# A third split product in two feature blocks of eight, kept high parts made at the ends of cycles, and four early transforms one product later

## Chip, cores, metric

One core of one Trainium2 chip runs the whole program. The metric is the device time of the program in microseconds; the smaller the better. Three runs of the kernel before gave 1777.51, 1778.03 and 1778.36 us, with a median of 1778.03 us.

## What is computed

The reference takes the real part of a two-dimensional Fourier transform of each of 8 sequences and runs every row of the result through a two-layer network with a hard swish between the layers:

```python
X = np.fft.fft(x, axis=1)          # x: 8 x 3008 x 256, fp32
X = np.fft.fft(X, axis=2)
x = X.real.astype(np.float32).reshape(8 * 3008, 256)
h = x @ w_in                       # 256 x 2048
g = h * np.clip(h + 3.0, 0.0, 6.0) / 6.0
out = g @ w_out                    # 2048 x 256
```

## The kernel before

**Tiling.** The 8 sequences are taken as 4 pairs (`NP`). The tokens of a pair are cut into 12 chunks (`NCK`), so there are 48 chunks; they are numbered 0 to 47 here. A chunk has 256 columns, the last of each pair (11, 23, 35, 47) has 192. The 2048 hidden features are cut into 8 feature blocks (`NF`) of 256. A **step** is one chunk with one feature block: 384 steps.

**A step.** TensorE makes the hidden values (`passes`, L717: split fp32 data in the tiles `KQ` and `KW`, fp32r matmuls), ScalarE and VectorE make the gate from them (`relu` L791, `other_sign` L751, `gate` L794, into `A`), GpSimd sums quarters of it (`combine`, L809, into `c`), and TensorE makes the second layer (`mlp2`, L865, into the PSUM tiles `acc`). The second layer is a 2x2 block product in seven products (a Strassen-like scheme): products 0, 1 and 2 take the gate itself, 3 to 6 take the sums `c`. So there are seven products to a step.

**Plain and split products.** A product in fp32 is one call and stands as two matmuls with two weight loads in the trace. From chunk 8 on (`CHUNK2`), products 0 and 1 of each step are split instead: the moving side is cut into a high, a low and a remaining part, and so is the weight, and three fp32r matmuls add up to the product. `split_gates` (L882) makes the moving parts in the tile `J`: ScalarE writes the high part (L886) and copies it into a PSUM bank (L891), VectorE writes the other two (L892, L893). In feature block 4 (`THIRD`), product 2 is split as well, in every chunk from 8 to 47: `split_third` (L896) does the same on one product's 256 columns (L900, L903, L904, L905) into `J3`.

**The weights' parts.** The second layer's weights of products 0 and 1 (and 2 in block 4) lie in `GH[fc]`, the others in `G` and `G2`. `split_weights` (L910) writes the low and remaining parts into `GK`. The high part takes the place of the fp32 weight in `GH`: `keep_high` (L921) copies `GH` into a PSUM bank (L924) and multiplies it back (L926), both on ScalarE. That can be done for a block when chunk 7 has used its fp32 weight, and has to be done before chunk 8 uses it.

**The order of the work.** The order on every engine is written out by hand in the main loop at the end of the kernel function. One turn of that loop is a **cycle**; from chunk 8 on a cycle is one step long. A cycle starts with the odd half of the hidden values (`odd_half`), then the first product, then the even half of the next unit (`passes(nx, 0)`), the gates, and the rest of the products. `products(n)` emits the next n products; of the last ones, `behind_it` come after the transform that stands in some cycles (`stage1`, L327, and `stage1_quarters`, the Fourier transform along the sequence, 8 matmuls of K=47). A second transform (`stage2`, L563, 8 short matmuls) stands in other cycles. High parts are made after the first product of the cycle before (`flush(high_of)`, `third_high`), other parts at the end of it (`third_others`). `keep_high` is called in the middle of a cycle, at most once in one, not in cycles with a transform, and not together with `split_weights`.

**PSUM banks.** Eight banks: four for `acc`, two (`a0`, `a1`) for the hidden values `u`, and `y0` and `y1`. `y0` holds the second sign `v` of the gate, the copies of `split_third`, and one half of a transform; `y1` holds the copies of `split_gates`, the bank of `keep_high` and `split_weights`, and the other half of a transform (`bank`, `other_bank`). While `keep_high` holds `y1`, `split_gates` goes to `y0` (`lent`).

Of the kernel before, what the change touches and what calls it, by code (L numbers as in the profile page):

```python
# [60 lines left out]
def kernel(  # L61
# [10 lines left out]
    nc = tc.nc  # L72
# [56 lines left out]
    CHUNK2, NFR = 8, 2  # L129
    THIRD = (4,)  # L130
    SPLIT = CHUNK1 * NF - 2
# [5 lines left out]
    F1 = consts.tile([P, 5 * PB], F32, name="F1")  # L137
    FI = consts.tile([P, NIX + 1 + P], F32, name="FI")
    IX = FI[:, 0:NIX].bitcast(I32)
# [4 lines left out]
    G = consts.tile([P, 6 - NFR, NF, P], F32, name="G")  # L144

    def split_products(fc):
        return NFR + (fc in THIRD)

    GH = [consts.tile([P, split_products(fc), P], F32, tag=f"GH{fc}", name="GH") for fc in range(NF)]
    G2 = {fc: consts.tile([P, P], F32, tag=f"G2{fc}", name="G2") for fc in range(NF) if fc not in THIRD}  # L150

    def weight(i, fc):
        if i == NFR and fc in G2:
            return G2[fc][:]
        return GH[fc][:, i] if i <= NFR else G[:, i - NFR - 1, fc]
    half = consts.tile([P, 1], F32, name="half")
# [673 lines left out]
    def split_of(ch, fc):  # L830
        return ch.n_all >= CHUNK2

    def order_of(ch, fc):

        if not split_of(ch, fc):
            return [[(i, None)] for i in range(7)]
        high, others = ([(i, j) for i in range(NFR)] for j in (HIGH, OTHERS))
        rest = [[(i, ALL if i < split_products(fc) else None)] for i in range(NFR, 7)]
        if ch.final and fc >= NF - LAST:
            return [high, others] + [rest[i - NFR] for i in (3, 5, 6, 4, 2)]  # L840
# [7 lines left out]
    def mlp2(ch, fc, lo, hi):  # L848
# [8 lines left out]
        for i, parts in (x for part in order[lo:hi] for x in part):  # L857
# [3 lines left out]
            for j in parts or (None,):  # L861
                assert (j is None) != (weight(i, fc).dtype == F32R)
                w = weight(i, fc) if not j else GK[fc][:, j - 1, i]
                x = moving[i] if j is None else J3[:, j, 0:ch.n] if i == NFR else parts_tile(ch, fc)[:, j, i, 0:ch.n]
                nc.tensor.matmul(o, w, x,  # L865
                                 start=(fc == 0 and i % 2 == 0 and j in (None, 0)), stop=(fc == NF - 1),
                                 skip_group_check=True)
# [42 lines left out]
    def split_weights(fc):  # L910

        low, rest = (GK[fc][:, k] for k in range(2))
        ps = bank([P, split_products(fc), P], "high")
        nc.scalar.mul(low, GH[fc][:], HIGH_PART)
        nc.vector.tensor_scalar(ps[:], low.bitcast(F32), 1.0 / EPS, None, op0=AL.mult)
        nc.vector.scalar_tensor_tensor(low, GH[fc][:], (1.0 + EPS) / EPS, ps[:], op0=AL.mult, op1=AL.subtract)
        nc.vector.scalar_tensor_tensor(ps[:], ps[:], -EPS, low.bitcast(F32), op0=AL.mult, op1=AL.add)
        yield
        nc.vector.tensor_scalar(rest, ps[:], 1.0 / (1.0 + EPS), None, op0=AL.mult)

    def keep_high(fc):  # L921

        ps = bank([P, split_products(fc), P], "high")
        nc.scalar.copy(ps[:], GH[fc][:])  # L924
        GH[fc] = consts.tile([P, split_products(fc), P], F32R, tag=f"GH{fc}", name="GH")
        nc.scalar.mul(GH[fc][:], ps[:], HIGH_PART)  # L926
        yield

# [173 lines left out]
    def join(j):  # L1102
# [7 lines left out]

        outs = GH[2 * n + i][:, 0:NFR], G[:, B12 - NFR - 1:B22 - NFR:B22 - B12, 2 * n + i]
        for h, o in enumerate(outs):
# [3 lines left out]
    def mix_w_out(j):  # L1116

        g = {i: G[:, i - NFR - 1, 2 * j:2 * j + 2, :] for i in range(NFR + 1, 7)}
        tt = nc.gpsimd.tensor_tensor
# [4 lines left out]
        for k in range(2):  # L1124
            tt(weight(2, 2 * j + k), g[5][:, k], GH[2 * j + k][:, B21], op=AL.subtract)

# [30 lines left out]


    def load_table():
        nc.sync.dma_start(out=F1[:], in_=c_stage1[:, 8 * PB:13 * PB])  # L1160
# [14 lines left out]
    load_w(0, nc.sync)  # L1175
    nc.scalar.dma_start(out=F[:], in_=c_stage1[:, 0:8 * PB])
    nc.scalar.dma_start(out=FI[:], in_=c_stage1[:, 13 * PB:])
    zero = QN[PB:PX, 2]
# [125 lines left out]
    def beside():  # L1304
# [5 lines left out]
        for t, gr in ((2, 2), (10, 3)):  # L1310
            put(t, load_t, gr)
        put(2, spread_half, halves[0], 1)
        put(5, load_table)
        put(NF - 1, close_w)
# [40 lines left out]
    def open_slots():  # L1355
        nonlocal A, GK
# [3 lines left out]
        GK = [slots.tile([P, 2, split_products(fc), P], F32R, tag=f"GK{fc}", name="GK") for fc in range(NF)]  # L1360

# [4 lines left out]

    epool = jpool = KW = A = GK = J = J3 = None
    steps = [(p, ck, fc) for p in range(NP) for ck in range(NCK) for fc in range(NF)]
# [256 lines left out]
    seed(units[1])  # L1625
    weights_of, rested, kept = list(range(NF)), 0, 0

# [3 lines left out]

    thirds = [s for s in gates_of if steps[s][2] in THIRD]
    third = []

    def third_high():

        if thirds and not third and thirds[0] <= now[0] + 1:
            ch, fc = chunk(thirds.pop(0))
# [50 lines left out]
    while done < len(stream):  # L1689
# [18 lines left out]
        third_high()  # L1708
        if not un:
            third_others()  # L1710

# [56 lines left out]
        flush(high_of)  # L1768
        third_others()
        for gen in parts:  # L1770
            next(gen, None)
# [112 lines left out]
```

## Time and profile before

| what | value |
| --- | --- |
| median of three runs | 1778.03 us |
| the profiled execution, whole | 1779.34 us |
| its span in the trace | 1777.5 us |
| TensorE busy | 1764.3 us |
| VectorE busy | 1494.5 us |
| ScalarE busy | 1411.4 us |
| GpSimd busy | 1312.7 us |
| granted clock of TensorE | 0.999 |

The profiled execution took 1.8 us more than its span and 1.3 us more than the median of the runs. TensorE's matmuls overlap in the trace, and their ends are modelled, so its busy time is close to the whole span also where it runs below its best. What a step costs is read better from the distance between the starts of two cycles: the first matmul of the odd half (L717 with 127 rows) marks the start of each.

### The profile page before, as it was taken

The numbers are of one execution on the slowest core, as the hardware profiler recorded it, in microseconds if no ns is written. First come the engines' busy times: TensorE is split into PE (matmuls) and PEld (weight loads), VectorE is DVE, ScalarE is ACT, GpSimd is POOL, SyncE is SP. The second block draws the span as 40 slices with busy tenths as digits, with TensorE's granted clock in tenths as the row PEclk, the third lists the DMA queues.
The fourth block names the chain that finished last, engine by engine and source line by source line (L and its number), as shares of the span: only waits on it lengthen the run. The fifth ranks groups of instructions, "written<-read, shape, count | busy, mean of one in ns | idle before, by whom it ended". The sixth has DMA issues, their size and how long they took to land.

```text
span 1777.5 us, 30218 instructions
## 1 busy us (share of the span) xinstructions
PE 1764.3 (99%) x9632; PEld 1518.3 (85%) x9632; DVE 1494.5 (84%) x2868; ACT 1411.4 (79%) x2573; POOL 1312.7 (74%) x1474
## 2 busy tenths in 40 slices
PE   8999999999999999999999999999999999999998
PEld 6688888888988888888998888888899888888897
DVE  8988676668988888888898888888899888888887
ACT  6556666678888888888888888888888888888885
POOL 5687777776678787886768878887766766776675
PEclk9999999999999999999999999999999999999999
DMA  8433332312113222121112222321111111101101
GB/s 281 121 93 99 103 78 70 85 37 51 37 48 81 71 64 78 47 73 43 30 44 64 70 78 57 86 64 37 48 36 34 37 21 48 41 19 45 21 13 34
DMA packets 160811, 110.39 MB, mean 62 GB/s; under 512 B 122562, under 2 KB 141344, under 8 KB 160652
## 3 DMA queue, kind: packets, MB, share of 16 engines
q1 hardware_dynamic: 151900, 82.22, 18.5%
q0 software_dynamic: 7504, 25.65, 4.7%
q8 instruction: 76, 1.25, 0.3%
q14 instruction: 83, 0.68, 0.1%
q10 hardware_dynamic: 1248, 0.59, 0.1%
HBM read 71.93 MB, written 36.79 MB: 61 GB/s over the span
## 4 chain that ended last, share of the span: by engine, by line
PE 95%; DVE 2%; ACT 2%; issue 0%; DMA 0%; another core or an unknown queue 0%; DVEq 0%; ACTq 0%
PE acc L865 58%; PE u L717 27%; PE ps L563 2%; PE ps L327 2%; PE acc L819 1%; PE v L613 1%; PE u L613 1%; ACT t L791 1%; PE spare L1138 0%; DVE v L751 0%; PE ps L526 0%; PE ps L395 0%; PE awake L1165 0%; DVE J L892 0%; ACT PM L1069 0%
## 5 line engine op out<-in xcount | busy, mean ns | idle before, releaser
L865 PE MATMUL acc<-c,G 128*128 128x256 f32 (+1 forms) x3008 | 766.7, 376 | 0.0
L717 PE MATMUL u<-KQ,KW 128*128 128x512 f32 (+7 forms) x2376 | 743.8, 426 | 1.0 <-ACT s L741 0.6
L809 POOL TENSOR_TENSOR c<-A 128x512 f32<-128x512 f32 (+1 forms) x359 | 453.9, 1264 | 337.3 <-PE acc L865 328.5
L865 PEld LDWEIGHTS acc<-c,G 128*128 128x128 f32 x3008 | 533.1, 189 | 80.3 <-issue 12.8
L717 PEld LDWEIGHTS u<-KQ,KW 128*128 128x128 f32 (+1 forms) x2376 | 426.1, 189 | 67.0 <-ACT s L741 3.0
L791 ACT ACTIVATE t<-u,half 128x512 f32<-128x512 f32 (+1 forms) x384 | 261.9, 682 | 169.9 <-PE u L717 111.7
L791 ACT ACTIVATE t<-v,half 128x512 f32<-128x512 f32 (+1 forms) x384 | 262.3, 683 | 106.1 <-DVE v L751 104.5
L751 DVE SCALAR_TENSOR_TENSOR v<-s,u 128x512 f32<-128x512 f32 (+1 forms) x360 | 247.0, 686 | 117.5 <-ACT t L791 111.6
L809 POOL TENSOR_TENSOR c<-c,A 128x256 f32<-128x256 f32 (+1 forms) x359 | 260.4, 725 | 28.2
L809 POOL TENSOR_TENSOR c<-A,c 128x256 f32<-128x256 f32 (+1 forms) x359 | 260.2, 725 | 28.2
L794 DVE SCALAR_TENSOR_TENSOR A<-t,v 128x512 f32<-128x512 f32 (+3 forms) x481 | 250.2, 541 | 36.7 <-ACT t L791 34.1
L865 PE MATMUL acc<-J,GK 128*128 128x256 f32 (+1 forms) x1340 | 270.7, 322 | 1.4 <-DVE J L905 0.8
L892 DVE SCALAR_TENSOR_TENSOR J<-high,A 128x512 fp32r<-128x512 f32 (+1 forms) x315 | 211.2, 670 | 55.8 <-ACT high L891 45.4
L794 DVE SCALAR_TENSOR_TENSOR A<-t,u 128x512 f32<-128x512 f32 (+3 forms) x481 | 248.4, 537 | 0.0
L732 ACT ACTIVATE u<-QN,WN 128x512 f32<-128x512 f32 (+1 forms) x324 | 224.8, 694 | 0.0
L865 PEld LDWEIGHTS acc<-J,GK 128*128 128x128 f32 x1340 | 204.7, 189 | 17.5 <-DVE J L893 1.6
L893 DVE SCALAR_TENSOR_TENSOR J<-high,A 128x512 fp32r<-128x512 f32 (+1 forms) x315 | 210.5, 668 | 0.0
L886 ACT ACTIVATE J<-A 128x512 fp32r<-128x512 f32 (+1 forms) x315 | 193.4, 614 | 0.0
L891 ACT COPY high<-J 128x512 f32<-128x512 f32 (+1 forms) x315 | 185.2, 588 | 4.9 <-DVE KQ L893 2.4
L741 ACT COPY s<-u 128x512 f32<-128x512 f32 (+2 forms) x315 | 180.3, 572 | 9.5 <-PE u L717 8.3
L865 PE MATMUL acc<-A,G 128*128 128x256 f32 (+1 forms) x630 | 184.6, 375 | 0.0
L865 PEld LDWEIGHTS acc<-J,GH 128*128 128x128 f32 x670 | 125.8, 189 | 24.1
(184 smaller groups left out, 1808.5 us busy)
## 6 DMA issues: line engine op xcount, KB each, us to landing
out_dram<-o SPq DMA_DIRECT2D x744, 32.0 KB
T<-in_c_stage_dram SPq DMA_DIRECT2D x26, 512.0 KB
g<-zd SPq DMA_DIRECT2D x42, 256.0 KB
zd<-z SPq DMA_DIRECT2D x48, 192.0 KB
QN<-qd SPq DMA_DIRECT2D x43, 128.0 KB
xt<-in_x_dram SPq DMA_DIRECT2D x21, 256.0 KB
st<-in_moe_w_out_dram POOLq DMA_DIRECT2D x7, 512.0 KB
xt<-in_x_dram SPq DMA_DIRECT2D x17, 192.0 KB
```

Of the source, the lines that this page charges most:

```text
L717: nc.tensor.matmul(un.wide(un.u[:]) if un.joint else un.u[:, i, 0:un.nq], un.weights(j, blk, i, rows), un.moving(j, blk, rows), start=Fals ...
L732: nc.scalar.activation(un.wide(un.u[:]), un.wide(row), AF.Identity, scale=WN[:, f:f + 1])
L741: copy(un.wide(un.s[:]), un.wide(un.u[:]))
L751: nc.vector.scalar_tensor_tensor(v, s, -2.0, u, op0=AL.mult, op1=AL.add)
L791: nc.scalar.activation(t, h, AF.Relu, bias=half[:], scale=scale)
L794: nc.vector.scalar_tensor_tensor(dst, t, 1.0, h, op0=AL.min, op1=AL.mult)
L809: (eng or nc.gpsimd).tensor_tensor(out, in0, in1, op=AL.add)
L865: nc.tensor.matmul(o, w, x, start=(fc == 0 and i % 2 == 0 and j in (None, 0)), stop=(fc == NF - 1), skip_group_check=True)
L886: nc.scalar.mul(high, a, 1.0 - EPS / 2.0)
L891: nc.scalar.copy(ps, high.bitcast(F32))
L892: nc.vector.scalar_tensor_tensor(low, ps, -1.0, a, op0=AL.mult, op1=AL.add)
L893: nc.vector.scalar_tensor_tensor(rest, ps, 1.0 + EPS, a, op0=AL.mult, op1=AL.subtract)
```

## The change

The change has five parts.

1. `THIRD` goes from block 4 to blocks 3 and 5, and a chunk that is the last of its pair has no third split product (`third_of`). So the third split products are those of blocks 3 and 5 in the 36 chunks from 8 on that aren't last, 72 in all, in place of 40 (block 4 in all 40 chunks).
2. `GH` holds two products for every block, `G` holds the other five, and the third product's weight parts lie in `GK3`, made by `split_third_weights` after the other weights. `split_weights` and it share `split_parts`.
3. `keep_high` takes `y0` in place of `y1`, is called at the end of a cycle, up to twice, and may start when two products of chunk 7's step are done in place of all seven. `split_gates` isn't moved to `y0` for it any more.
4. Before step 62 a transform stands before the last product of its cycle, not before the last two (`behind_it`).
5. To make room in SBUF: the row that `split_q` sends out lies in `QN`, and the index and sign columns `FI` are loaded a second time into `signs` at step 2 (`load_index`, one DMA on SyncE's queue), since the first copy now lies in a pool that is closed early.

```diff
-    THIRD = (4,)
+    THIRD = (3,5)
...
+    def third_of(ch, fc):
+        return split_of(ch, fc) and fc in THIRD and not ch.last
...
-        if fc in THIRD:
-            rest = rest[1:3] + rest[0:1] + rest[3:]
+        rest = [[(i, None)] for i in range(NFR, 7)]
+        if third_of(ch, fc):
+            rest = rest[1:3] + [[(NFR, ALL)]] + rest[3:]
         order = [high] + rest[:2] + [others] + rest[2:]
...
+    def split_third_weights(fc):
+        yield from split_parts(weight(NFR, fc), bank([P, P], "high")[:], *(GK3[fc][:, j] for j in range(3)))
...
     def keep_high(fc):
 
-        ps = bank([P, split_products(fc), P], "high")
+        ps = ps_u.tile([P, NFR, P], F32, tag="y0", name="high")
         nc.scalar.copy(ps[:], GH[fc][:])
-        GH[fc] = consts.tile([P, split_products(fc), P], F32R, tag=f"GH{fc}", name="GH")
+        GH[fc] = consts.tile([P, NFR, P], F32R, tag=f"GH{fc}", name="GH")
         nc.scalar.mul(GH[fc][:], ps[:], HIGH_PART)
-        yield
...
-        ch.row = qpool.tile([P, TB], F32, tag="row", name="row")
+        ch.row = QN[:, ch.n_all % 4]
...
+    def load_index():
+        nonlocal FI, IX
+        FI, IX = signs, signs[:, 0:NIX].bitcast(I32)
+        nc.sync.dma_start(out=FI[:], in_=c_stage1[:, 13 * PB:13 * PB + NIX + 1])
...
     def third_others():
+        third_high()
         for gen in third:
             next(gen, None)
...
-        if kept < NF and not stages and not ends and done >= 7 * ((CHUNK2 - 1) * NF + kept - SPLIT) + 7:
-            splitting, kept = keep_high(kept), kept + 1
-            next(splitting)
-        elif weights_of and not stages and not ends and not closing and rested >= 3:
-            splitting, rested = split_weights(weights_of.pop(0)), 0
+        if weights_of and not stages and not ends and not closing and rested >= 3:
+            (f, fc), rested = weights_of.pop(0), 0
+            splitting = f(fc)
             next(splitting)
         lent[0] = splitting is not None
-        behind_it = 1 if any(s - 1 in middle_fns for s in begun) else 2
+        behind_it = 1 if any(s - 1 in middle_fns or s < CHUNK2 * NF - 2 for s in begun) else 2
...
         third_others()
+        for _ in range(2):
+            if kept < NF and not stages and not ends and done >= 7 * ((CHUNK2 - 1) * NF + kept - SPLIT) + NFR:
+                keep_high(kept)
+                kept += 1
```

Three places show how instructions move. The first is ScalarE around the start of chunk 8, before the change. `COPY high<-GH` and `ACTIVATE GH<-high` are one `keep_high`, `J<-A` and `high<-J` the split of the gates, `t` the two `relu`, `s` and `u` the hidden values of the next step.

```order
L741 COPY s<-u 128x512
L791 ACTIVATE t<-v,half 128x512
L924 COPY high<-GH 128x384
L926 ACTIVATE GH<-high 128x384
L891 COPY high<-J 128x512
L732 ACTIVATE u<-QN,WN 128x512
L791 ACTIVATE t<-u,half 128x512
L886 ACTIVATE J<-A 128x512
L791 ACTIVATE t<-v,half 128x512
L741 COPY s<-u 128x512
L924 COPY high<-GH 128x256
L926 ACTIVATE GH<-high 128x256
```

The same place on ScalarE after the change, from chunk 8's first step on:

```order
L733 COPY s<-u 128x512
L783 ACTIVATE t<-v,half 128x512
L889 COPY high<-J 128x512
L724 ACTIVATE u<-QN,WN 128x512
L927 COPY high<-GH 128x256
L929 ACTIVATE GH<-high 128x256
L927 COPY high<-GH 128x256
L929 ACTIVATE GH<-high 128x256
L783 ACTIVATE t<-u,half 128x512
L884 ACTIVATE J<-A 128x512
```

Before, the last four of the eight `keep_high` stand in the first four cycles of chunk 8, each ahead of `high<-J` and the next `u`; after, the last two stand behind `u` in the first of these cycles, the other six stand earlier, and the following cycles have none.

The second place is TensorE at the first transform after the hidden values are split, before (`ps` are the two banks of the transform, `y` its data):

```order
L865 MATMUL acc<-A,GH 128x256
L865 MATMUL acc<-A,G_112 128x256
L327 MATMUL ps_1871<-y,F_97 64x512
L327 MATMUL ps_1872<-y,F_97 64x512
L327 MATMUL ps_1871<-y,F_97 64x512
L327 MATMUL ps_1872<-y,F_97 64x512
L865 MATMUL acc<-c,G 128x256 x2
L717 MATMUL u<-KQ,KW 128x256 x6
```

The same place after:

```order
L863 MATMUL acc<-A,GH 128x256
L863 MATMUL acc<-A,G 128x256
L863 MATMUL acc<-c,G 128x256
L319 MATMUL ps_1860<-y,F_97 64x512
L319 MATMUL ps_1861<-y,F_97 64x512
L319 MATMUL ps_1860<-y,F_97 64x512
L319 MATMUL ps_1861<-y,F_97 64x512
L863 MATMUL acc<-c,G 128x256
```

One product `acc<-c,G` has moved from behind the transform to the front of it; the same happens at three more transforms and at no others.

The third place is ScalarE in a late chunk, before, around the third product of block 4 (`J<-A 128x256` and `high<-J 128x256`):

```order
L791 ACTIVATE t<-u,half 128x512
L886 ACTIVATE J<-A 128x512
L900 ACTIVATE J<-A 128x256
L791 ACTIVATE t<-v,half 128x512
L741 COPY s<-u 128x512
L891 COPY high<-J 128x512
L732 ACTIVATE u<-QN,WN 128x512
L903 COPY high<-J 128x256
```

After, from the second half of block 3's set to just ahead of block 5's:

```order
L783 ACTIVATE t<-v,half 128x512
L733 COPY s<-u 128x512
L889 COPY high<-J 128x512
L724 ACTIVATE u<-QN,WN 128x512
L901 COPY high<-J 128x256
L783 ACTIVATE t<-u,half 128x512
L884 ACTIVATE J<-A 128x512
L783 ACTIVATE t<-v,half 128x512
L733 COPY s<-u 128x512
L889 COPY high<-J 128x512
L724 ACTIVATE u<-QN,WN 128x512
L783 ACTIVATE t<-u,half 128x512
```

The set of two small operations stands once in a chunk before, in the cycle of block 3; after, it stands twice, in the cycles of blocks 2 and 4, and the cycle between (from the first `t<-u` of these rows to the last `u`) has none.

More of the change, by code (lines that the diff above doesn't have):

```diff
@@ L143 @@
     WN = consts.tile([P, NFC], F32, name="WN")
[L144 to L150, printed above, removed]
+    G = consts.tile([P, 7 - NFR, NF, P], F32, name="G")
+    GH = [consts.tile([P, NFR, P], F32, tag=f"GH{fc}", name="GH") for fc in range(NF)]
     def weight(i, fc):
-        if i == NFR and fc in G2:
-            return G2[fc][:]
-        return GH[fc][:, i] if i <= NFR else G[:, i - NFR - 1, fc]
+        return GH[fc][:, i] if i < NFR else G[:, i - NFR, fc]
     half = consts.tile([P, 1], F32, name="half")
@@ L837, in order_of @@
         high, others = ([(i, j) for i in range(NFR)] for j in (HIGH, OTHERS))
-        rest = [[(i, ALL if i < split_products(fc) else None)] for i in range(NFR, 7)]
         if ch.final and fc >= NF - LAST:
-            return [high, others] + [rest[i - NFR] for i in (3, 5, 6, 4, 2)]
-        if fc in THIRD:
-            rest = rest[1:3] + rest[0:1] + rest[3:]
+            return [high, others] + [[(i, None)] for i in (3, 5, 6, 4, 2)]
+        rest = [[(i, None)] for i in range(NFR, 7)]
+        if third_of(ch, fc):
+            rest = rest[1:3] + [[(NFR, ALL)]] + rest[3:]
         order = [high] + rest[:2] + [others] + rest[2:]
@@ L861, in mlp2 @@
             for j in parts or (None,):
-                assert (j is None) != (weight(i, fc).dtype == F32R)
-                w = weight(i, fc) if not j else GK[fc][:, j - 1, i]
-                x = moving[i] if j is None else J3[:, j, 0:ch.n] if i == NFR else parts_tile(ch, fc)[:, j, i, 0:ch.n]
+                w, x = weight(i, fc), moving[i]
+                if parts and i == NFR:
+                    w, x = GK3[fc][:, j], J3[:, j, 0:ch.n]
+                elif parts:
+                    w, x = GK[:, j - 1, fc, i] if j else w, parts_tile(ch, fc)[:, j, i, 0:ch.n]
+                assert (j is None) != (w.dtype == F32R)
                 nc.tensor.matmul(o, w, x,
@@ L910, in split_weights, with split_parts @@
     def split_weights(fc):
[L912 to L917 removed]
+        low, rest = (GK[:, k, fc] for k in range(2))
+        yield from split_parts(GH[fc][:], bank([P, NFR, P], "high")[:], low, low, rest)
+    def split_third_weights(fc):
+        yield from split_parts(weight(NFR, fc), bank([P, P], "high")[:], *(GK3[fc][:, j] for j in range(3)))
+    def split_parts(w, ps, high, low, rest):
+        nc.scalar.mul(high, w, HIGH_PART)
+        nc.vector.tensor_scalar(ps, high.bitcast(F32), 1.0 / EPS, None, op0=AL.mult)
+        nc.vector.scalar_tensor_tensor(low, w, (1.0 + EPS) / EPS, ps, op0=AL.mult, op1=AL.subtract)
+        nc.vector.scalar_tensor_tensor(ps, ps, -EPS, low.bitcast(F32), op0=AL.mult, op1=AL.add)
         yield
[L919 removed]
+        nc.vector.tensor_scalar(rest, ps, 1.0 / (1.0 + EPS), None, op0=AL.mult)
     def keep_high(fc):
[L923 removed]
+        ps = ps_u.tile([P, NFR, P], F32, tag="y0", name="high")
         nc.scalar.copy(ps[:], GH[fc][:])
[L925 removed]
+        GH[fc] = consts.tile([P, NFR, P], F32R, tag=f"GH{fc}", name="GH")
         nc.scalar.mul(GH[fc][:], ps[:], HIGH_PART)
[L927 removed]
     HIGH_PART = (1.0 + EPS) * (1.0 - EPS / 2.0)
@@ L1116, in mix_w_out @@
     def mix_w_out(j):
-        g = {i: G[:, i - NFR - 1, 2 * j:2 * j + 2, :] for i in range(NFR + 1, 7)}
+        g = {i: G[:, i - NFR, 2 * j:2 * j + 2, :] for i in range(NFR, 7)}
         tt = nc.gpsimd.tensor_tensor
@@ L1359, in open_slots @@
         A = slots.tile([P, NSLOT, 2, 2, TB], F32, name="A")
-        GK = [slots.tile([P, 2, split_products(fc), P], F32R, tag=f"GK{fc}", name="GK") for fc in range(NF)]
+        GK = slots.tile([P, 2, NF, NFR, P], F32R, name="GK")
+        GK3 = {fc: slots.tile([P, 3, P], F32R, tag=f"GK{fc}", name="GK3") for fc in THIRD}
     def open_parts():
@@ L1625 @@
     seed(units[1])
-    weights_of, rested, kept = list(range(NF)), 0, 0
+    weights_of = [(split_weights, fc) for fc in range(NF)] + [(split_third_weights, fc) for fc in THIRD]
+    rested, kept = 0, 0
     def turn_before(s):
         return s - (3 if chunk(s)[0].final and steps[s][2] else 1)
-    thirds = [s for s in gates_of if steps[s][2] in THIRD]
+    thirds = [s for s in gates_of if third_of(*chunk(s))]
     third = []
```

17 lines of the change are left out of this document (9 added, 8 removed).

## Prediction

> **What bounds the kernel now.** I read the page first, for the engine that sets the end.
>
> ```profile
> span 1777.5 us, 30218 instructions
> PE 1764.3 (99%) x9632; PEld 1518.3 (85%) x9632; DVE 1494.5 (84%) x2868; ACT 1411.4 (79%) x2573; POOL 1312.7 (74%) x1474
> PE 95%; DVE 2%; ACT 2%; issue 0%; DMA 0%; another core or an unknown queue 0%; DVEq 0%; ACTq 0%
> L865 PEld LDWEIGHTS acc<-c,G 128*128 128x128 f32 x3008 | 533.1, 189 | 80.3 <-issue 12.8
> ```
>
> TensorE is 99% busy and 95% of the chain of waits. So a gain has to come out of TensorE's own work, or out of the few places where it stands still. Second, I cut one late chunk (chunk 40, no transform `stage1` any more) into its steps, in the view of busy time by stretch; the columns are length, then the busy time of PE, PEld, DVE, ACT, POOL.
>
> ```profile
> 1509.55:1513.80 4.25, 4.25 (x24) 3.72 (x23) 4.15 (x10) 4.09 (x9) 2.77 (x3) 1.00 0.12 27
> 1522.31:1526.57 4.26, 4.26 (x24) 3.74 (x23) 3.56 (x8) 3.75 (x8) 3.11 (x4) 1.00 0.01 4
> 1526.57:1530.75 4.18, 4.18 (x26) 3.71 (x24) 3.88 (x8) 3.49 (x7) 2.76 (x3) 1.00 0.18 40
> 1530.75:1535.89 5.14, 5.14 (x32) 4.62 (x31) 3.65 (x7) 4.62 (x10) 2.76 (x3) 1.00 0.10 22
> 1535.89:1540.15 4.26, 4.26 (x24) 3.74 (x23) 4.26 (x8) 3.44 (x7) 2.77 (x3) 1.00 0.41 118
> 1540.15:1544.41 4.26, 4.26 (x25) 3.73 (x23) 4.05 (x9) 3.35 (x7) 2.77 (x3) 1.00 0.25 73
> ```
>
> These are blocks 0, 3, 4, 5, 6, 7. A step takes 4.25 to 4.26 us; block 5's has `stage2` in it. The one step with a third split product (block 4) takes 4.18 us, and TensorE is full in all of them. VectorE is nearly full in blocks 6, 7 and 0, and has room in blocks 2 to 5.
>
> **Term 1: the third split products.** 36 chunks get one more of them: 36 x (4.26 - 4.18) = 2.9 us less on TensorE. That difference already holds the third weight load. What the set adds elsewhere (two operations on ScalarE, two on VectorE):
>
> ```profile
> L900 ACT ACTIVATE J<-A 128x256 fp32r<-128x256 f32 x36 | 14.6, 405 | 0.0
> L903 ACT COPY high<-J 128x256 f32<-128x256 f32 x36 | 13.4, 372 | 0.7 <-DVE J L893 0.7
> ...
> 1527.73 0.41 DVE L904 SCALAR_TENSOR_TENSOR J<-high,A 128x256 fp32r<-128x256 f32 x1
> 1528.06 0.41 DVE L905 SCALAR_TENSOR_TENSOR J<-high,A 128x256 fp32r<-128x256 f32 x1
> ...
> 1531.61 0.68 DVE L893 SCALAR_TENSOR_TENSOR J<-high,A 128x512 fp32r<-128x512 f32 x1
> 1532.56 0.70 DVE L751 SCALAR_TENSOR_TENSOR v<-s,u 128x512 f32<-128x512 f32 x1 [0.27 <-ACT t L791]
> ...
> 1535.86 0.69 DVE L892 SCALAR_TENSOR_TENSOR J<-high,A 128x512 fp32r<-128x512 f32 x1 [0.81 <-ACT high L891]
> ```
>
> ScalarE gets 0.41 + 0.37 = 0.78 us, in cycles in which it has 0.5 us (block 3's, which held a set) and more free. On VectorE the operations start 0.33 us apart, so a set takes 0.66 us. Block 5's set is queued behind L893 at 1531.61 and ahead of `v` at 1532.56, which waited 0.27 us anyway: `v` comes 0.66 - 0.27 = 0.39 us later, and behind it the gates, the second `relu`, and the copy of `u` for which TensorE's next odd half waits. The 0.81 us that VectorE waits at 1535.86 are there to take up most of that. Block 3's set stands in block 2's cycle and meets cycles with as much room as block 3's own. Bounds of this term: 2.9 us if all is hidden; 1.5 us if every chunk gives 0.04 us back. I take 2.9, since the step with a set is the nearest row and shows it hidden.
>
> By the Trainium skill, "FP8 and Floating Point Precision", section "TensorE Precision Notes", a true fp32 product is four passes through the array, a reduced one a single pass. With the gap of N/2.4 + 2.5 ns for a matmul that "TensorE: Matmul & The Clock Gate" states in "Back-to-back issue gap", I estimate that three passes for four save 0.109 us at 256 columns, and 36 of them 3.9 us; the steps above show 0.08, so I keep 2.9.
>
> **Term 2: last chunks without a third split product.** Here are blocks 3 and 4 of chunk 11.
>
> ```profile
> 497.55:501.26 3.71, 3.71 (x25) 3.39 (x23) 3.36 (x11) 3.52 (x8) 2.43 (x4) 1.00 0.03 7
> 501.26:505.36 4.10, 3.96 (x26) 3.41 (x24) 3.83 (x10) 3.44 (x8) 2.27 (x4) 1.00 0.14 31
> ...
> 1763.62 0.35 DVE L904 SCALAR_TENSOR_TENSOR J<-high,A 128x192 fp32r<-128x192 f32 x1
> 1763.88 0.34 DVE L905 SCALAR_TENSOR_TENSOR J<-high,A 128x192 fp32r<-128x192 f32 x1
> 1764.15 0.76 DVE L1015 STREAM_TRANSPOSE o<-e 128x256 f32<-128x256 f32 x2
> ...
> 1764.28 0.47 PE L865 MATMUL acc<-J,GK 128*128 128x192 f32 x2 [0.84 <-DVE J L905]
> ```
>
> With 192 columns the step with a set is longer, 4.10 us for 3.71, with TensorE idle in it. Three such chunks (11, 23, 35) save 3 x 0.39 = 1.2 us. In the final chunk, 47, TensorE waits 0.84 us for L905. VectorE gets rid of the 0.53 us from 1763.62 to 1764.15, and what follows it there is next in line; I take 0.5 us (bounds 0 and 0.84). Sum 1.7 us.
>
> **Term 3: `keep_high`.** Chunks 8 and 20 hold the same work for TensorE (211 and 212 records, the difference is a lost one); I set them side by side, then two single steps of chunk 8, and the waits in it.
>
> ```profile
> 379.08:417.65 38.57, 37.94 (x211) 31.61 (x209) 30.67 (x54) 32.22 (x63) 27.61 (x33) 1.00 0.16 42
> 807.23:844.05 36.82, 36.82 (x212) 31.98 (x210) 30.90 (x56) 30.47 (x57) 24.04 (x26) 1.00 0.17 43
> ...
> 383.36:387.61 4.25, 4.25 (x24) 3.67 (x23) 3.30 (x6) 3.83 (x8) 4.09 (x7) 1.00 0.02 6
> 387.61:392.10 4.49, 4.49 (x24) 3.66 (x23) 3.25 (x7) 4.04 (x9) 4.33 (x8) 1.00 0.00 0
> ...
> PEld u L717 <- ACT u L732: 1.1, 3, 0.4
> PEld u L717 <- ACT s L741: 1.0, 1, 1.0
> ...
> L924 ACT COPY high<-GH 128x256 f32<-128x256 f32 x7 | 2.7, 390 | 0.0
> L926 ACT ACTIVATE GH<-high 128x256 fp32r<-128x256 f32 x7 | 2.7, 385 | 0.2
> ```
>
> Chunk 8 takes 38.57 - 36.82 = 1.75 us more, and TensorE's waits there are for ScalarE's `u` and `s`. Four `keep_high` of 0.39 + 0.39 = 0.78 us stand ahead of them. Moved away, that is gone. What takes their place: two `keep_high` in a row, 1.56 us, behind `u` of chunk 8's first cycle, with the next `relu` queued behind them. A step with one costs 4.49 - 4.25 = 0.24 us, so two cost some 0.4 (bounds 0 and 1.56). The six earlier ones stand behind `u`, where ScalarE waits for TensorE. 1.75 - 0.4 = 1.4 us (bounds 0.2 and 1.75).
>
> **Term 4: four transforms one product later.** Busy time of the transform's matmuls (L327) alone, in the four cycles that change, and in a later one; then TensorE's wait for their second bank, and a cycle with six plain products beside one with seven.
>
> ```profile
> 181.11:187.35 6.24, 2.10 (x8) 0.39 (x8) 1.00 0.35 123
> 200.30:206.20 5.90, 1.76 (x8) 0.39 (x8) 1.00 0.39 99
> 263.72:269.89 6.17, 2.03 (x8) 0.39 (x8) 1.00 0.68 165
> 303.62:309.41 5.79, 1.69 (x8) 0.39 (x8) 1.00 0.01 3
> 593.08:598.86 5.78, 1.40 (x8) 0.39 (x8) 1.00 0.01 3
> ...
> PEld ps L327 <- DVE A L794: 2.8, 5, 0.8
> ...
> 206.20:210.21 4.01, 4.01 (x27) 3.69 (x25) 1.99 (x4) 2.45 (x5) 3.85 (x4) 1.00 0.77 239
> 210.21:214.65 4.44, 4.44 (x28) 4.07 (x27) 2.45 (x5) 3.11 (x8) 4.28 (x6) 1.00 0.25 70
> ```
>
> The excess over 1.40 us is 0.70, 0.36, 0.63 and 0.29 us: the bank `y0` is still read by the gate (L794). A product of 4.44 - 4.01 = 0.43 us in front fills of it 0.43 + 0.36 + 0.43 + 0.29 = 1.5 us (bounds 0.7, if the next cycle is then late, and 1.6).
>
> The rest costs nothing that I can find: the second load of the index columns is one DMA on SyncE's queue, 128 rows of 33 numbers, in a stretch where that queue is waiting; the row of `split_q` is the same copy into another tile; the two `split_third_weights` stand in chunks 6 and 7, where VectorE is busy 2 of 4 us (206.20).
>
> **The sum.** 2.9 + 1.7 + 1.4 + 1.5 = 7.5 us. The profiled execution, 1779.34, becomes 1771.8; the median of the runs stands 1.3 us below it, 1778.0, and becomes **1770.5 us**.
>
> **Rivals.** *VectorE passes its lateness on (slower).* Its blocks 6, 7 and 0 are 4.26, 4.05 and 4.15 us full. If the 0.39 us of block 5's set isn't taken up by the 0.81 us wait, it goes through these three steps and TensorE waits at each chunk's start: 36 x 0.39 = 14.0 us, so 1778.0 - 7.5 + 14.0 = 1784.5. It decides from the point where `v` of block 6 is later than the 0.2 us that block 7 has free. For it: three full steps in a row. Against: the 0.81 us wait lies ahead of them. 7%.
>
> *Weight loads beside the matmuls don't hide (near no change).* A load takes 0.189 us in its row, and a split product has three for two. If these were paid in line, a set would cost 0.189 - 0.08 = 0.11 us and not save 0.08: 1778.0 - 7.5 + 2.9 + 4.0 = 1777.4. Against it: block 4's step has the three loads and is the shorter one. 2%. The Trainium skill says in "TensorE: Matmul & The Clock Gate", "The mechanism", that a weight load overlaps matmuls in flight only if it goes to other rows of the array, and here all loads take 128 rows; the trace disagrees, with 85% of the span busy in loads beside 99% in matmuls.
>
> *The third products bring nothing*, since another engine paces the steps that get them: 1778.0 - 4.6 = 1773.4. Against it: TensorE is full in blocks 3 and 5. 12%.
>
> *The early waits only move* (terms 3 and 4 come back at the next `u`): 1778.0 - 4.6 = 1773.4. For it: ScalarE is the pacer in chunk 8. 15%.
>
> That the change doesn't do what it says is excluded by the order of its instructions.
>
> **How the numbers follow.** The forecast has 64%, the rivals the rest. About 0.2%, 3.6 us, is what a measurement of this kernel can tell from no change. Faster (below 1774.5): the forecast, the two rivals at 1773.4, less what of them falls beyond: 86%. Same: 8%, of it 2% the loads. Slower: 6%. The bounds of the four terms add up to 1.5 + 0.9 + 0.2 + 0.7 = 3.3 and 2.9 + 2.0 + 1.75 + 1.6 = 8.3 us, so 1774.7 and 1769.7; with the unsure half microsecond between executions at both ends the range is 1769.0 to 1775.2, and it holds both rivals at 1773.4.
>
> **What would show it.** Blocks 3 and 5 at 0.08 us less than before and block 4 at 4.26; block 4 of chunk 11 at about 3.71; chunk 8 below 37.4 us with no wait for `u` past its second step; L327 busy near 1.4 to 1.7 us in the four early cycles. A wait of TensorE for `s` at the start of blocks 6, 7 or 0, in every chunk, would prove the first rival.

## The result, and the profile after

The changed kernel takes **1769.72 us** (median of 6 runs, 1769.18 to 1770.73) for 1778.07 us before (6 runs): a ratio of 0.9954 with an interval of 0.9943 to 0.9966, 8.35 us less. The forecast was 1770.5. The profiled execution took 1770.73 us for a span of 1769.0 us.

The page of the changed kernel, its span, its engines and its chain of waits by engine:

```profile
span 1769.0 us, 30458 instructions
PE 1759.5 (99%) x9664; PEld 1518.5 (86%) x9664; DVE 1514.2 (86%) x2940; ACT 1430.1 (81%) x2639; POOL 1312.6 (74%) x1474
PE 97%; DVE 1%; ACT 1%; DMA 1%; issue 0%; ACTq 0%; DVEq 0%
```

TensorE is still 99% busy, and its share of the chain went from 95 to 97%: DVE and ACT, 2% each before, have 1% each. Of the 8.5 us that the span lost by these rows (8.6 unrounded, 1777.54 less 1768.96), 4.8 are TensorE's busy time (which holds some of its waits, as in the transform's matmuls below); the rest was standing still.

I cut both traces into steps, at the first matmul of each odd half, and compared step with step. Chunk 40 of the changed kernel, blocks 0, 3, 4, 5, 6 and 7, in the view by stretch:

```profile
1502.15:1506.40 4.25, 4.25 (x24) 3.72 (x23) 4.15 (x10) 4.09 (x9) 2.76 (x3) 1.00 0.14 32
...
1514.92:1519.10 4.18, 4.18 (x26) 3.73 (x24) 3.91 (x9) 3.48 (x7) 3.10 (x4) 1.00 0.00 0
1519.10:1523.34 4.24, 4.24 (x24) 3.72 (x23) 3.54 (x7) 4.01 (x9) 2.76 (x3) 1.00 0.16 37
1523.34:1528.42 5.08, 5.08 (x34) 4.63 (x32) 4.26 (x8) 4.38 (x9) 2.76 (x3) 1.00 0.10 23
1528.42:1532.66 4.24, 4.24 (x24) 3.72 (x23) 4.00 (x7) 3.52 (x7) 2.77 (x3) 1.00 0.33 86
1532.66:1536.92 4.26, 4.26 (x24) 3.74 (x23) 4.26 (x9) 3.54 (x8) 2.77 (x3) 1.00 0.31 101
```

Block 3 went from 4.26 to 4.18 us, block 4 from 4.18 to 4.24, block 5 from 5.14 to 5.08; blocks 6, 7 and 0 stayed within 0.02. Next, blocks 3 and 4 of chunk 11, all of chunk 8, and in it the step with two `keep_high`:

```profile
493.69:497.40 3.71, 3.71 (x24) 3.39 (x22) 3.35 (x11) 3.27 (x7) 2.43 (x4) 1.00 0.02 4
497.40:501.12 3.72, 3.72 (x24) 3.40 (x22) 3.30 (x8) 3.27 (x7) 2.21 (x3) 1.00 0.12 27
...
376.98:413.94 36.96, 36.96 (x212) 31.86 (x210) 31.03 (x56) 31.44 (x61) 27.64 (x33) 1.00 0.17 44
...
381.25:385.82 4.57, 4.57 (x25) 3.71 (x23) 3.09 (x6) 4.23 (x10) 4.41 (x7) 1.00 0.02 5
```

Block 4 of chunk 11 takes 3.72 us for 4.10. Chunk 8 takes 36.96 us for 38.57, although its second step, behind the two `keep_high`, takes 4.57 for 4.25. Most of the gain, 1.3 us, is in the step of its block 4, which took 5.59 us before and takes 4.27 now. Last, the early transform's matmuls (L319 in the changed kernel) in their four cycles:

```profile
180.93:186.73 5.80, 1.66 (x8) 0.39 (x8) 1.00 0.37 125
...
199.67:205.14 5.47, 1.33 (x8) 0.39 (x8) 1.00 0.41 104
262.48:268.21 5.73, 1.60 (x8) 0.39 (x8) 1.00 0.79 178
301.94:307.31 5.37, 1.25 (x8) 0.37 (x8) 1.00 0.01 3
```

Each of the four cycles is shorter by 0.42 to 0.44 us, the length of the one product put in front. Summed over the steps (in us, from the two traces):

| part | predicted | measured |
|---|---|---|
| 1, third products, chunks 9 to 46 without last ones (block 3 -2.50, block 4 +2.60, block 5 -2.86) | -2.9 | -2.8 |
| 2, last chunks (3 x 0.38) and what follows the last odd half | -1.7 | -1.1 - 0.6 |
| 3, chunk 8 (of it 0.08 by its third set) | -1.4 | -1.6 |
| 4, four early transforms | -1.5 | -1.7 |
| not predicted: the step at 249.7 us -0.2, ahead of the first odd half -0.2, scattered -0.4 | 0 | -0.8 |
| sum | -7.5 | -8.6 |

### The profile page after: what moved, and what is told of

It is laid out like the page before. It is cut to its first block, busy times and chain, and to the rows that moved or that the text cites. A ratio compares the mean times of both kernels' runs of the same rounds, so it can differ in the third digit from the quotient of the medians.

```text
span 1769.0 us, 30458 instructions
## 1 busy us (share of the span) xinstructions
PE 1759.5 (99%) x9664; PEld 1518.5 (86%) x9664; DVE 1514.2 (86%) x2940; ACT 1430.1 (81%) x2639; POOL 1312.6 (74%) x1474
## 3 DMA queue, kind: packets, MB, share of 16 engines
q8 instruction: 76, 1.25, 0.3%
## 4 chain that ended last, share of the span: by engine, by line
PE 97%; DVE 1%; ACT 1%; DMA 1%; issue 0%; ACTq 0%; DVEq 0%
PE acc L863 60%; PE u L709 28%; PE ps L555 2%; PE ps L319 2%; PE acc L811 1%; PE v L605 1%; PE u L605 1%; PE spare L1140 0%; DMA xt<-in_x_dram,IT 0%; ACT PM L1071 0%; PE ps L518 0%; PE ex L1085 0%; DMA QN<-in_x_dram 0%; PE wps L1140 0%; PE ps L425 0%
## 5 line engine op out<-in xcount | busy, mean ns | idle before, releaser
L863 PE MATMUL acc<-J,GK 128*128 128x256 f32 (+1 forms) x1476 | 282.3, 319 | 0.5 <-DVE J L891 0.5
L786 DVE SCALAR_TENSOR_TENSOR A<-t,v 128x512 f32<-128x512 f32 (+3 forms) x481 | 249.7, 539 | 36.9 <-ACT t L783 34.3
L890 DVE SCALAR_TENSOR_TENSOR J<-high,A 128x512 fp32r<-128x512 f32 (+1 forms) x315 | 210.6, 669 | 52.2 <-ACT high L889 46.9
L863 PEld LDWEIGHTS acc<-J,GK 128*128 128x128 f32 x1476 | 217.9, 189 | 16.4 <-DVE J L891 1.1
L891 DVE SCALAR_TENSOR_TENSOR J<-high,A 128x512 fp32r<-128x512 f32 (+1 forms) x315 | 210.0, 667 | 0.0
L863 PE MATMUL acc<-A,G 128*128 128x256 f32 (+1 forms) x576 | 168.2, 374 | 0.0
L863 PEld LDWEIGHTS acc<-J,GH 128*128 128x128 f32 x630 | 118.3, 189 | 23.7
```

Of the source, the lines that this page charges most:

```text
L786: nc.vector.scalar_tensor_tensor(dst, t, 1.0, h, op0=AL.min, op1=AL.mult)
L863: nc.tensor.matmul(o, w, x, start=(fc == 0 and i % 2 == 0 and j in (None, 0)), stop=(fc == NF - 1), skip_group_check=True)
L890: nc.vector.scalar_tensor_tensor(low, ps, -1.0, a, op0=AL.mult, op1=AL.add)
L891: nc.vector.scalar_tensor_tensor(rest, ps, 1.0 + EPS, a, op0=AL.mult, op1=AL.subtract)
```

## The experiments

There were eleven runs: nine edited kernels, one of them twice, and the changed kernel once more. Each was timed beside the kernel before on its own chip (1777.72, 1777.69 and 1778.07 us in the three groups), so times of different groups compare to some 0.4 us. Where nothing else is said, an edit is to the changed kernel.

### The two halves apart

**thirds_only**: terms 1 and 2 alone.

```diff
-        behind_it = 1 if any(s - 1 in middle_fns or s < CHUNK2 * NF - 2 for s in begun) else 2
+        behind_it = 1 if any(s - 1 in middle_fns for s in begun) else 2
...
-        for _ in range(2):
-            if kept < NF and not stages and not ends and done >= ... + NFR:
-                keep_high(kept)
...
+        if kept < NF and not stages and not ends and done >= ... + 7:
+            splitting, kept = keep_high(kept), kept + 1
...
-        ps = ps_u.tile([P, NFR, P], F32, tag="y0", name="high")
+        ps = bank([P, NFR, P], "high")
```

> The changed kernel with keep_high back in its old place and the four early transforms back behind two products: what is left of the change is the third split products in blocks 3 and 5, none in last chunks. Theory (four separate terms): the third products save 36 x 0.077 us, the last chunks 1.1 us, the final chunk 0.4 us, so 1778.1 - 4.3 = 1773.8 us. Rival (the third products bring nothing, only the last chunks do): 1776.6. Rival (the gain is all in the early part): 1778.

Measured: 1773.26 us, ratio 0.9974 (0.9963 to 0.9984), 4.5 us less than before. The theory's 4.3 holds; both rivals are outside the interval. In its trace the long step of chunk 8 has moved with the third set: block 3 takes 5.59 us, as block 4 did before. There a `keep_high` stands ahead of the copy `high<-J` of the gates, and the set's own copy waits 0.74 us behind it. So a `keep_high` costs most where it meets a third set. Chunk 8 as a whole is 0.35 us longer than before, 0.28 of it in block 6.

**early_only**: terms 3 and 4 alone.

```diff
-    THIRD = (3,5)
+    THIRD = (4,)
...
-        return split_of(ch, fc) and fc in THIRD and not ch.last
+        return split_of(ch, fc) and fc in THIRD
```

> The changed kernel with the third split product in block 4 of every chunk from 8 on, last chunks too, as before: what is left is keep_high in its new place and the four early transforms one product later. Theory: chunk 8 gives 1.6 us, the four transforms 4 x 0.43 = 1.7 us, so 1778.1 - 3.3 = 1774.8 us, at most 0.5 us less if the small gains ahead of 181 us and at 249 us are real. Rival (the early waits only move): 1778. The two parts should add up to the whole change: 4.3 + 3.3 = 7.6, or 8.1 with the small gains, of 8.35.

Measured: 1777.76 us, ratio 0.9998 (0.9989 to 1.0007). No gain: by the time alone, the rival. But in its trace the four early cycles and chunk 8 are as short as in the changed kernel (1.73 and 1.60 us less), and the loss stands in the final chunk, where the part behind the last odd half is 3.1 us longer. TensorE's wait there, and the time behind it by stretch, with the granted clock of TensorE third from the right:

```profile
1761.76 0.47 PE L863 MATMUL acc<-J,GK 128*128 128x192 f32 x2 [2.43 <-DVE J L903]
...
1762.20:1765.70 3.50, 3.50 (x18) 3.50 (x16) 0.60 (x2) 0.00 (x0) 0.74 (x2) 0.51 0.25 56
1765.70:1770.00 4.30, 4.30 (x31) 4.30 (x30) 1.91 (x6) 0.61 (x2) 0.00 (x0) 1.00 0.04 9
```

Before, this wait was 0.84 us, so it is 1.6 us longer. The other half of the loss comes behind it: for 3.5 us the clock is 0.51, and the matmuls up to 1767.02 take 1.5 us longer than the same ones before. In the kernel before and in the next run, with waits of 0.84 and 0.83 us at this place, the clock stays at 1.00.

The change also deletes a line that made the set's second half early in cycles without a new `u`; without a set in the final chunk nothing needs that line, but my edit put the set back there and left the line out. VectorE now makes the set behind the sums of that cycle. So this run tested my edit and not the theory. The next run is early_only with these lines put back:

```diff
+        if not un:
+            third_others()
```

> As early_only, but in the cycles without a new product of u (the final chunk) the second half of the third set stands again ahead of the sums, as it did before the change. Theory (early_only lost its gain in the final chunk alone, where TensorE waited 2.4 us for the set instead of 0.84): the 3.3 us come back, 3.5 with the gain at 249 us: 1774.3 us against 1777.7 before. Rival (the early waits only move, and the final chunk was by the way): no change against before, 1777.7.

Measured (**early_mended**): 1774.84 us, ratio 0.9984 (0.9975 to 0.9993), 2.9 us less than before; from the first odd half to the last its trace is 3.2 us shorter. The early waits are gone for good: behind chunk 8 its steps are longer than before by only some 0.3 us in all, scattered. The halves give 4.5 + 2.9 = 7.4 of 8.35 us; the intervals (1.6 to 1.9 us to either side of each) allow them to add up. In the traces they fall somewhat short too: chunk 8 is 0.35 us longer in thirds_only, which the whole change doesn't pay, and the rest is scattered.

### What a third set is worth, and where it costs

A set here means the four small operations, two on ScalarE and two on VectorE, that split the gates of one third product.

**no_thirds**: `THIRD = ()`.

> The changed kernel with no third split product at all; block 3's, 4's and 5's third products are plain in every chunk. Theory (72 sets at 0.077 us each, nothing given back): 5.5 us more than the changed kernel, 1775.2 us. Rival (the sets give part of it back on VectorE, 0.04 us in a chunk): 1773.8. Rival (a set saves what three passes for four would, 0.109 us, in the steps, and other places take it back): 1777.6 at most.

Measured: 1775.94 us, 6.2 us more than the changed kernel, ratio to before 0.9988 (0.9979 to 0.9997). From the first odd half to the last it is 5.9 us longer: 5.9 / 72 = 0.08 us for a set. In the changed kernel's trace an fp32r matmul of 256 columns starts 0.119 us (median) behind the one before it, and the matmuls of plain products, two to a product, start 0.216 us apart: 2 x 0.216 - 3 x 0.119 = 0.075 us, close to the set's gain. Its blocks 3 and 6 of chunk 40 both have full length, 4.26 and 4.25 us. The Trainium skill, "TensorE: Matmul & The Clock Gate", section "Back-to-back issue gap", gave the estimate of 0.109 us for a set in the prediction, 7.8 us for 72; the run shows less, and the measurement decides.

**thirds_35last**: sets in last chunks too (the second edit of early_only).

> The changed kernel with the sets of blocks 3 and 5 in last chunks too, which before had one in block 4. Theory (in a last chunk ScalarE and VectorE pace a step, and a set costs them 0.38 us): block 3 of chunks 11, 23 and 35 pays 3 x 0.38 = 1.1 us, block 5 as much or, since TensorE has stage2 in it, nothing; in the final chunk block 3 pays some 0.5 us and up to 3 us, as its set's second half now stands behind the sums. 1769.7 + 1.6 to 5 us, so 1771.3 to 1774.7. Rival (a set saves 0.06 us in a last chunk too): 1769.3.

Measured: 1772.62 us, 2.9 us more than the changed kernel, ratio to before 0.9973 (0.9963 to 0.9983). Blocks 3 and 6 of its chunk 11:

```profile
492.36:496.45 4.09, 3.95 (x26) 3.40 (x24) 3.88 (x13) 3.43 (x8) 2.48 (x5) 1.00 0.02 4
...
504.80:509.08 4.28, 4.17 (x27) 3.55 (x26) 3.58 (x8) 3.69 (x9) 2.23 (x4) 1.00 0.21 31
```

Block 3's set costs 0.38 us, as expected. Block 5's costs nothing in block 5 and 0.34 us in block 6 (3.94 us in the changed kernel): its lateness is paid one step later. 3 x (0.38 + 0.34) = 2.2 us, and 0.7 us behind the last odd half.

**low_twice**: one more VectorE operation in block 5's set.

```diff
-        nc.vector.scalar_tensor_tensor(low, ps, -1.0, a, op0=AL.mult, op1=AL.add)
+        for _ in range(1 + (fc == 5)):
+            nc.vector.scalar_tensor_tensor(low, ps, -1.0, a, op0=AL.mult, op1=AL.add)
```

> The changed kernel in which block 5's set does its first VectorE operation twice, 0.33 us more on VectorE in 36 chunks; nothing else changes, the result neither. In the changed kernel's chunk 40 TensorE's next even half at the start of block 7 finds its s ready 0.29 us early (0.49 before the change), and 0.55 us early at the chunk's end. Theory (the lateness of v in block 5 is carried over blocks 6 and 7 and there eaten up): 0.33 - 0.29 = 0.04 us in a chunk, 1769.7 + 1.5 = 1771.2 us. Rival (the 0.81 us for which VectorE waits at block 6 take it all up, as the prediction had it): 1769.7. Rival (every lateness passes on): 36 x 0.33 = 11.9, 1781.6.

Measured: 1774.69 us, ratio to before 0.9982 (0.9973 to 0.9991): 5.0 us more than the changed kernel, where the theory had 1.5 and its rivals 0 and 11.9. TensorE and then VectorE in chunk 40 of this kernel, blocks 6 and 7 from 1532.21 on:

```profile
1532.21:1536.65 4.44, 4.44 (x24) 3.70 (x22) 3.74 (x7) 3.71 (x8) 2.77 (x3) 1.00 0.28 64
1536.65:1540.82 4.17, 4.17 (x23) 3.67 (x23) 4.17 (x8) 3.68 (x8) 2.77 (x3) 1.00 0.35 118
```

```profile
1528.32 0.87 DVE L903 SCALAR_TENSOR_TENSOR J<-high,A 128x256 fp32r<-128x256 f32 x2
1529.11 0.41 DVE L904 SCALAR_TENSOR_TENSOR J<-high,A 128x256 fp32r<-128x256 f32 x1
...
1532.91 0.69 DVE L890 SCALAR_TENSOR_TENSOR J<-high,A 128x512 fp32r<-128x512 f32 x1 [0.79 <-ACT high L889]
```

Two things are to be seen. The place is the theory's: block 6 is 0.20 us longer (block 7 then 0.09 shorter), with TensorE waiting for ScalarE's `s` in 36 places (9.2 us, for 1.0 us in 4 places in the changed kernel). The size was mine to get wrong: an operation that writes the same tile again starts 0.46 us after the first (0.87 less 0.41), not 0.33. With a room of 0.31 us (worked out under term 1 below) that makes 0.46 - 0.31 = 0.15 us in a chunk, 36 x 0.15 = 5.4 us. It agrees in the sum more than in its parts: most chunks pay about 0.11 us, and chunks 10, 22 and 34, each ahead of a last one, 0.6 us. And the wait ahead of L890, 0.81 us before the change, is still 0.79 us: it takes up nothing.

**thirds_67**: `THIRD = (6,7)`.

> The changed kernel with the third split products in blocks 6 and 7 instead of 3 and 5: as many products, but their sets stand in steps in which VectorE is full. Theory (room on VectorE decides what a set costs): 0.66 us in block 6 against 0.49 us of room at block 7's start, so 0.17 us, and 0.66 us more in block 7 against what is left there, some 0.4 us; 36 x 0.56 = 20 us, so about 1790 us, between 1780 and 1796. Rival (VectorE's room does not matter, a set always saves 0.08 us): 1769.7.

Measured: 1808.23 us, ratio to before 1.0166 (1.0152 to 1.0180): the theory's sign and place, 18 us above its number and outside its bounds. Blocks 6 and 7 of chunk 40, and TensorE's waits that are longest in sum:

```profile
1563.16:1567.71 4.55, 4.54 (x25) 3.71 (x23) 4.45 (x9) 3.34 (x7) 2.76 (x3) 1.00 0.45 129
1567.71:1572.48 4.77, 4.48 (x23) 3.64 (x23) 4.67 (x10) 4.12 (x9) 2.97 (x4) 1.00 0.16 44
```

```profile
PEld u L709 <- DVE s L733: 24.3, 36, 1.0
PEld u L709 <- ACT s L733: 12.5, 35, 0.4
```

Without a set these steps are 4.25 and 4.26 us. Summed over all chunks from 8 on, blocks 6 and 7 are 26 us longer than in no_thirds, the blocks 0 that follow 5 us, and blocks 3 and 5 no longer save their 5.9 us. What was too small is the price of a set. It is read in the trace of the next kernel, and of the changed one alike: from the start of the set's first operation to the start of `v` it is 0.84 to 0.85 us.

**thirds_56**: `THIRD = (5,6)`, run to test that correction.

> The changed kernel with the third split products in blocks 5 and 6 instead of 3 and 5. The corrected rule, from the runs so far: a set keeps VectorE from v for 0.85 us (from the start of its first operation to the start of v), not 0.66, and what exceeds the room of 0.32 us that s has at block 7's start when block 5 holds a set is paid in full. 0.85 - 0.32 = 0.53 us in each of 36 chunks, 19 us: 1789 us. By the prediction's 0.66 us: 0.34 us in a chunk, 12 us, 1782. Rival (only sets in neighbouring blocks at the chunk's end cost): 1770 to 1775.

Measured: 1791.18 us, ratio to before 1.0071 (1.0056 to 1.0087): 21.5 us more than the changed kernel, where the corrected price gives 19 and the prediction's 12. Block 6 of chunk 40, and VectorE and ScalarE in it:

```profile
1545.75:1550.55 4.80, 4.54 (x25) 3.70 (x23) 4.49 (x9) 4.01 (x9) 2.94 (x4) 1.00 0.42 125
```

```profile
1547.76 0.41 DVE L902 SCALAR_TENSOR_TENSOR J<-high,A 128x256 fp32r<-128x256 f32 x1
1548.09 0.41 DVE L903 SCALAR_TENSOR_TENSOR J<-high,A 128x256 fp32r<-128x256 f32 x1
1548.61 0.70 DVE L743 SCALAR_TENSOR_TENSOR v<-s,u 128x512 f32<-128x512 f32 x1
```

```profile
1549.34 0.69 ACT L783 ACTIVATE t<-v,half 128x512 f32<-128x512 f32 x1 [0.40 <-DVE v L743]
1549.92 0.58 ACT L733 COPY s<-u 128x512 f32<-128x512 f32 x1
```

The step is 4.80 us for 4.24: 0.56 for the expected 0.53. (The sum of 19 us left out that block 3, which gave up its set, is longer again: 2.5 us in all.) The chain is in the rows: set, `v`, second `relu`, copy `s` until 1550.50, and TensorE's odd half at 1550.55. Between L903 and `v` lie 0.52 us where L902 and L903 are 0.33 apart. The set's copy and `v` use the same PSUM bank `y0`, so `v` starts only when L903 has ended (1548.50); that this is the reason is argued, no run gave them separate banks.

### One more product in front

**behind_none**: the early transforms' second half behind all products.

```diff
-        behind_it = 1 if any(s - 1 in middle_fns or s < CHUNK2 * NF - 2 for s in begun) else 2
+        behind_it = 1 if any(s - 1 in middle_fns for s in begun) else 0 if any(s < CHUNK2 * NF - 2 for s in begun) else 2
```

> The changed kernel with the early transforms' second half behind all products of the cycle, one more product in front of it than now. In the changed kernel the transform's matmuls are busy 1.66, 1.33, 1.60 and 1.25 us in the four cycles; if the last is the floor, 0.41 + 0.08 + 0.35 = 0.84 us are left there. Theory (a product in front fills of the wait whatever is left): 1769.7 - 0.8 = 1768.9 us, and 1.25 us busy in each of the four. Rival (the transform's results, now later, hold up the next cycle): 1769.7 or up to 1.7 us more, since all four then move.

Measured: 1768.16 us, ratio to before 0.9948 (0.9935 to 0.9962). L319 in the four cycles:

```profile
180.87:186.32 5.45, 1.16 (x8) 0.35 (x8) 1.00 0.38 133
...
199.16:204.47 5.31, 1.01 (x8) 0.21 (x8) 1.00 0.41 109
261.73:267.11 5.38, 1.09 (x8) 0.28 (x8) 1.00 0.91 211
300.76:306.05 5.29, 1.02 (x8) 0.21 (x8) 1.00 0.02 3
```

These are 0.50, 0.32, 0.51 and 0.23 us less, the floor lies near 1.0 and not at 1.25, and the cycles are 0.35, 0.16, 0.35 and 0.08 us shorter. The cycle behind each is 0.07 to 0.10 us shorter too, so 1.3 us is gone there, and 1.1 us from the first odd half to the last. To see it in the time, both ran once more on one chip (**after_again** is the changed kernel unedited, **behind_again** is behind_none):

> The changed kernel once more, to stand beside the next one on the same chip: 0.9954 of the time before, about 1769.7 us.

> behind_none once more, beside the changed kernel on the same chip. Theory (the profile's 0.95 us in four cycles is a gain for good): 0.9 us less than the changed kernel, which so many runs tell apart barely. Rival: no difference.

Measured: 1769.48 us, ratio 0.9950 (0.9936 to 0.9963), and 1769.19 us, ratio 0.9944 (0.9931 to 0.9958). The cycles are shorter by the same amounts again, but the times don't tell the two apart. It is the fastest version of the study by its trace, not shown by its time.

## Why the prediction was right, point by point

**The number.** The measured 1769.72 us stands right where the upper bounds of all four terms together put it (1769.7). The terms themselves gave 7.8 us for 7.5; the other 0.8 us was in no term, and that it left the time inside the range is luck.

**What bounds it.** Right as far as causes are known: TensorE's own work and its few stops gave the 7.8 us.

**Term 1** was right in size (2.8 for 2.9 us; no_thirds gives 0.08 us for each of 72 sets), so the rival that the third products bring nothing is out. So is the rival of the weight loads: had they been paid in line, no_thirds would be the faster kernel, and it is 6.2 us slower. (The loads of the second layer take 128 rows, as it says; those of the odd half take 127 and the transforms' 47.) The *cover* of term 1 was named wrongly. The prediction let block 5's `v` come 0.39 us late and had VectorE's 0.81 us wait at block 6 take it up. VectorE in the changed kernel, blocks 5 to 7 of chunk 40, then ScalarE's copy `s` in block 6:

```profile
1523.93 0.68 DVE L891 SCALAR_TENSOR_TENSOR J<-high,A 128x512 fp32r<-128x512 f32 x1
1524.53 0.41 DVE L902 SCALAR_TENSOR_TENSOR J<-high,A 128x256 fp32r<-128x256 f32 x1
...
1525.37 0.70 DVE L743 SCALAR_TENSOR_TENSOR v<-s,u 128x512 f32<-128x512 f32 x1
...
1528.66 0.69 DVE L890 SCALAR_TENSOR_TENSOR J<-high,A 128x512 fp32r<-128x512 f32 x1 [0.80 <-ACT high L889]
...
1530.47 0.69 DVE L743 SCALAR_TENSOR_TENSOR v<-s,u 128x512 f32<-128x512 f32 x1
...
1534.46 0.70 DVE L743 SCALAR_TENSOR_TENSOR v<-s,u 128x512 f32<-128x512 f32 x1
...
1535.66 0.68 DVE L733 COPY s<-u 128x512 f32<-128x512 f32 x1
```

```profile
1531.77 0.58 ACT L733 COPY s<-u 128x512 f32<-128x512 f32 x1
```

And of before, the same places in blocks 6 and 7 (VectorE's `v` and `s`, ScalarE's `s`):

```profile
1537.74 0.70 DVE L751 SCALAR_TENSOR_TENSOR v<-s,u 128x512 f32<-128x512 f32 x1
...
1541.96 0.70 DVE L751 SCALAR_TENSOR_TENSOR v<-s,u 128x512 f32<-128x512 f32 x1 [0.21 <-ACT t L791]
...
1543.16 0.68 DVE L741 COPY s<-u 128x512 f32<-128x512 f32 x1
```

```profile
1539.06 0.58 ACT L741 COPY s<-u 128x512 f32<-128x512 f32 x1
```

Counted from each step's start, block 5's `v` comes at 2.03 us for 1.81 before: 0.22 late. Two errors met here. The set takes 0.85 us and not 0.66; and L891 starts at 0.59 us for 0.86, because block 4 has no set any more, which the prediction forgot (0.58 us in no_thirds, 0.84 in early_mended, whose set is in block 4). That the second error outweighed the first was luck. The 0.8 us wait at block 6 does not shrink: what ends it is ScalarE's `high`, which stands behind ScalarE's work on that same late `v`. So the lateness goes on: block 6's `v` is 0.20 us late (2.05 for 1.85), and ScalarE's `s` ends at 1532.35, 0.31 us ahead of TensorE's odd half at 1532.66, where before it was 0.51 (1539.64 to 1540.15). Block 7 takes it up: its wait of 0.21 us ahead of `v` is gone, `v` is on time (1.80 for 1.81), and so is the copy `s` (3.00 for 3.01). That is the very 0.2 us that the first rival named as its point of decision, reached to the hundredth, with 0.3 us of TensorE's own room behind it. Low_twice (5.0 us), thirds_56 (21.5) and thirds_67 (38.5) show what lies past it. The rival was nearer than its 7% said.

**Term 2** was right: 3 x 0.38 us for 3 x 0.39, and 0.6 for 0.5 behind the last odd half. (The sum of the lower bounds takes 0.9 us for it, where its own bounds give 1.2.)

**Term 3** was right: 1.6 us for 1.4, with 0.08 of it the third set. The two `keep_high` in a row cost 0.3 us (4.57 for 4.25), for which 0.4 was taken. In chunk 8 TensorE no longer waits for `u`, and for `s` only once, 0.4 us behind the second step. The price of 0.24 us that the prediction read for one `keep_high` holds for the steps without a third set's copy; the 1.3 us of block 4 came in through the difference of whole chunks.

**Term 4** was somewhat small: 1.7 us for 1.5, above its own upper bound of 1.6. The step that was off is the floor of the transform's matmuls. A late cycle's 1.40 us was taken for it; in the kernel before the transform from 334.53 us on takes 1.09, and behind_none reaches 1.0 us in the early ones. So all four cycles had more to fill than a product is long, and each won the whole 0.43 us. Early_mended shows that this and term 3 are not given back, which the second rival near 1773.4 would have had. The late cycles may hold some of this wait too, but no run moved a late transform.

**The rest**, 0.8 us, was not predicted. The step at 249.7 us is 0.18 us shorter in thirds_only and in early_mended too; I found no cause for it and tried none.

## What to carry to other kernels

A wait in front of an operation is room only if what ends the wait does not itself hang on the late work: follow the releaser back before you spend the gap. The room that counts is between the end of the last operation that the bounding engine needs and the moment when it needs it (0.31 us here), and work is charged to it from the first start to the next user's start (0.85 us), not by the spacing of like operations (0.66). A wait can cost the bounding engine more than its length: behind early_only's 2.43 us the clock was 0.51 for 3.5 us. A part of a change that is run alone must keep the lines that the other part made unnecessary.

## What the hardware showed beside that

The part ahead of the first odd half differs between executions of the same instructions. In three executions, the changed kernel twice (after, after_again) and behind_again, whose first 180 us are the same, the stretch from 20 to 40 us, with the granted clock in the third column from the right:

```profile
20.00:40.00 20.00, 19.15 (x91) 13.47 (x88) 15.40 (x30) 13.62 (x27) 8.85 (x12) 0.91 0.89 308
```

```profile
20.00:40.00 20.00, 18.55 (x88) 12.91 (x87) 15.83 (x32) 14.66 (x26) 9.59 (x13) 1.00 0.87 307
```

```profile
20.00:40.00 20.00, 17.40 (x71) 12.92 (x72) 11.71 (x23) 10.41 (x19) 8.73 (x12) 0.83 0.81 285
```

The clock there is 0.91, 1.00 and 0.83, and the first odd half comes at 167.1, 165.7 and 170.6 us. In shorter stretches it is 0.51 from 20.0 to 23.5 us in the first execution and 0.51 from 27.8 to 34.7 us in the third, and 1.00 beside that. From there to the last odd half the changed kernel takes 1575.4 and 1575.5 us, and behind_none and behind_again 1574.3 and 1574.1. So nearly all of the difference between executions of one kernel arises ahead of its first odd half, and a change of less than a microsecond is better read from the steps than from the time. What lowers the clock was not tested. An idle TensorE stands ahead of it in early_only (2.43 us) and in behind_again (1.94 us until 26.83), but behind_none stands idle there for 1.84 us and keeps 1.00, and the changed kernel's drop at 20.0 us has no idle time of 1 us ahead of it.
